# Pool's K and V loads as one transfer per kv-head, even heads first

## The chip, the cores and the metric

The kernel runs on one core of one Trainium2 chip. The metric is the device time of one execution in microseconds; the time before is the median of three runs. A profile of one execution, with its trace, stands beside the times.

## The reference

One decode step (one token, batch of 4) of an attention block and a GeGLU block that share a layer norm and are added to the input, together with the gradients of everything. With `D` = 512, 32 query heads, 8 kv-heads, `Dh` = 128, a cache of 4096 rows of which the last `W` = 1024 are attended, and an FFN width of 1792, cut to what matters:

```python
def _A_ref(x, k_cache, v_cache, wq, wo):
    W = min(4096, max(256, Sk // 4))
    q = (x @ wq).reshape(B, Sq, Hq, Dh).transpose(0, 2, 1, 3)
    k = jnp.repeat(k_cache[:, :, Sk - W:, :], rep, axis=1)
    v = jnp.repeat(v_cache[:, :, Sk - W:, :], rep, axis=1)
    p = softmax(einsum("bhqd,bhkd->bhqk", q, k) * Dh ** -0.5)
    return einsum("bhqk,bhkd->bhqd", p, v).transpose(0, 2, 1, 3).reshape(B, Sq, Hq * Dh) @ wo
def _B_ref(x, w_gate, w_up, w_down):
    return (gelu(x @ w_gate) * (x @ w_up)) @ w_down
xn = layernorm(x)
y = x + _A_ref(xn, k_cache, v_cache, wq, wo) + _B_ref(xn, w_gate, w_up, w_down)
# outputs: y, and the gradients for x, k_cache, v_cache, wq, wo, w_gate, w_up, w_down under grad_out
```

All tensors are bf16. The gradients of the caches have the caches' full shape, 32 MiB each. Outside of the window of 1024 rows they are zero, so 48 MiB of zeros are written; inside it stand dK and dV, 16 MiB in all. The kernel reads the windows of K and V, 8 MiB each.

## The kernel before, in words

The program works in three stages. First comes the FFN, forward and backward, with its weight gradients; in the meantime `wq`, `wo` and the first batch's K arrive on SP's queue. Then comes the attention, one batch after another. At the end are the projections' outputs and the gradients of `wo` and `wq`, in eight stores of 1 MiB.

K and V of a batch are tiles of 128 partitions by 8 kv-heads by 8 rows by 128 columns (2 MiB). A partition `m` holds the 8 consecutive cache rows `8m` to `8m+7` of each head, so one head is 2 KB on each partition, and one contiguous 256 KB in the cache. The pieces of a batch's work, in the names that the prediction uses:

- `load_kv` (L216) allocates the tile and issues its transfers (L222) at high priority. The first K load (`ka`) is issued by SP; the other seven by Pool (GpSimd): V of all four batches (`va`, one buffer), K of batches 1 to 3 (`kb`, `ka`, `kb`). The V load of the next batch waits until TensorE has finished its products with the old V (`odq`, tile `od_ps`), as it takes the same buffer; K loads wait likewise.
- `refill` (L462) copies the query rows, or the rows of the output's gradient, into the block-diagonal operands `bd` (tiles `D3q` and `D3d` are the sources) on Pool. The four `bd` tiles are cleared by memsets (L392) on Pool before their first use.
- `scores` (L471) makes the products with K (`S`) or V (`dP`). VectorE transposes 32x32 blocks of the tile into a scratch tile (`scr`, two buffers, L93), and TensorE multiplies it with `bd` into `sc_ps`. There are four transposes for a tile: two over the even heads, then two over the odd ones.
- `softmax`, `turned`, `odq` and `softmax_d` make the probabilities, the outputs and the gradient of the scores. `odq` reads the K or V tile head by head.
- `dvdk` (L550) makes dV or dK of a batch: products into `kv_ps`, copies by ScalarE and VectorE (`evac`, L88 and L89) into two of the four staging buffers `stg`, and two stores of 1 MiB each on Pool's queue (`result`, L106). A staging buffer can be written again when its store has landed.
- `zeros` (L236) issues the zero stores, 32 of 1.5 MiB, on SP's queue. Their order is written out by hand (SP is the only engine whose order is): a zero store waits for the landing of the second or third one before it, and in many places for the landing of the load that `load_kv` returned, which is the last transfer that it created:

```python
zeros(2, load_kv(0, 1, att, "va", nc.gpsimd, single_packet=True))
zeros(3, load_kv(1, 0, att, "kb", nc.gpsimd, single_packet=True))
```

The order on the other engines, Pool among them, is made by the Tile scheduler from priorities and a model of costs; each engine then runs its instructions in that order. Semaphores are assigned afterwards by Tile: landings of Pool's transfers are counted on eight semaphores taken in turn.

Of the kernel before, what the change touches and what calls it, by code (L numbers as in the profile page):

```python
# [18 lines left out]
def kernel(  # L19
# [24 lines left out]
    nc = tc.nc  # L44

    B, Sq, D = A_x.shape
    _, G, Sk, Dh = A_k_cache.shape
# [168 lines left out]
    def load_kv(b, k, pool, tag, eng, **kw):  # L216
        d_, src = ((k_t, A_k_cache), (v_t, A_v_cache))[k]
        tl = pool.tile([P, G, J, Dh], BF16, name=tag, tag=tag)
        for hf in range(2):
            hs = slice(hf * G // 2, (hf + 1) * G // 2)  # L220
            with tc.high_priority():
                d = eng.dma_start(out=tl[:, hs].rearrange("p g j d -> p g (j d)"),  # L222
                                  in_=src[b, hs, K0:Sk, :].rearrange("g (m j) d -> m g (j d)", j=J), **kw)
        d_[b] = tl
        return d
# [23 lines left out]
    with tc.tile_pool(name="ffn", bufs=1) as ffn:  # L249
# [17 lines left out]
        nc.sync.dma_start(out=wq_sb[:].rearrange("p c n -> p (c n)"), in_=A_wq.rearrange("(p c) n -> p (c n)", c=C))  # L267
        nc.sync.dma_start(out=wo_sb[:].rearrange("p k n -> p (k n)"), in_=A_wo.rearrange("(p k) n -> p (k n)", k=KH))
        load_kv(0, 0, kap, "ka", nc.sync)
        zeros(4)  # L270

# [103 lines left out]
    with tc.tile_pool(name="mid", bufs=1, reuse_waits="tile") as mid:  # L375
# [3 lines left out]
        selb = mid.tile([Q, 4, P], BF16, name="selb")  # L379
        with tc.tile_pool(name="att", bufs=1, reuse_waits="tile") as att:  # L380
            zeros(2, load_kv(0, 1, att, "va", nc.gpsimd, single_packet=True))
            zeros(3, load_kv(1, 0, att, "kb", nc.gpsimd, single_packet=True))


# [381 lines left out]
```

## Time and profile before

| What | Value |
|---|---|
| Median of 3 runs | 285.05 us (284.68 to 286.16) |
| The profiled execution | 284.82 us, span 283.0 us, 4400 instructions |
| Bytes moved | 112.21 MB, mean 396 GB/s over the span |
| Read and written in HBM | 30.93 MB and 81.01 MB |
| Pool's loads (`va`, `kb`, `ka`) | 8 + 4 + 2 transfers of 1024 KB, median 17.6, 19.4 and 13.0 us from issue to landing |
| Stores of dK, dV and the last two gradients | 24 of 1024 KB, median 13.7 us |
| Zero stores | 32 of 1536 KB, median 12.1 us |
| Granted TensorE clock, mean | 0.603 |

Rows of a timeline are: start in us, duration in us, engine, line, operation, output and input tiles, shape, number of instructions, and in brackets the idle time before it and what ended that. A "q" behind an engine's name is its sequencer. The queues' rows are packets, MB, and the time that the packets took as a share of sixteen DMA engines over the span (q1 is SP's, q0 Pool's). The slices divide the span into 40 equal parts, each digit a busy share in tenths.

### The profile page before, as it was taken

The page shows a single profiled execution, that of the slowest core. Times are in us where ns is not written, and L with a number is a line of the kernel's source. Part 1 is how long each engine was busy: PE and PEld are TensorE (multiplying, and loading weights), DVE is VectorE, ACT ScalarE, POOL GpSimd, SP SyncE. Part 2 cuts the span into 40 slices and gives each one's busy share as a digit, 9 for nine tenths or more (in the row PEclk, how much of TensorE's full clock was granted, in tenths as well). Part 3 has the DMA queues.
Part 4 walks back from the last instruction along what each step waited for, and adds up shares of the span by engine and source line. Part 5 has one row for each costly group of instructions (what it writes and reads, how often), then busy time and mean ns, then how long its engine had stood idle before and what let it go on. Part 6 is the DMA issues. An engine that isn't in the chain of part 4 may idle for free.

```text
span 283.0 us, 4400 instructions
## 1 busy us (share of the span) xinstructions
PE 187.6 (66%) x1731; PEld 76.8 (27%) x1733; DVE 165.0 (58%) x309; ACT 124.4 (44%) x245; POOL 60.3 (21%) x135
## 2 busy tenths in 40 slices
PE   0225989859544899759976663923357998944870
PEld 0102344233111543234331341311034232510210
DVE  4779674898798533635257254055496104396970
ACT  2032774740010469744725420802432767454870
POOL 8500000169075313120040060200020020201110
PEclk9999965556955555755555555555555555685555
DMA  6999989999999999999999999999999999999995
GB/s 217 430 446 435 432 317 420 424 430 396 392 428 406 383 357 425 328 365 411 421 419 414 408 427 405 396 422 421 429 382 423 413 410 403 399 415 396 391 397 223
DMA packets 16883, 112.21 MB, mean 396 GB/s; under 512 B 1368, under 2 KB 1632, under 8 KB 11104
## 3 DMA queue, kind: packets, MB, share of 16 engines
q1 hardware_dynamic: 6544, 66.46, 57.0%
q0 software_dynamic: 10176, 45.35, 40.8%
q8 instruction: 13, 0.21, 0.3%
q10 hardware_dynamic: 144, 0.13, 0.2%
q14 instruction: 6, 0.05, 0.0%
HBM read 30.93 MB, written 81.01 MB: 396 GB/s over the span
## 4 chain that ended last, share of the span: by engine, by line
DMA 30%; issue 14%; PE 13%; DVE 9%; ACT 3%; POOL 2%; POOLq 0%; ACTq 0%; DVEq 0%
DMA out_dram<-stg 30%; DVE scr L93 4%; PE kv_ps L117 4%; PE od_ps L117 3%; PE sc_ps L117 2%; PE dwq_ps L117 2%; ACT stg L88 2%; DVE stg L89 1%; POOL out_dram L106 1%; PE ok_ps L117 1%; PE es_ps L117 1%; DVE spr L492 1%; DVE dqs L593 1%; ACT E_f L524 1%; PE nm_ps L117 1%
## 5 line engine op out<-in xcount | busy, mean ns | idle before, releaser
L88 ACT CAST stg<-kv_ps 128x512 bf16<-128x512 f32 x118 | 63.6, 606 | 52.2 <-DMA out_dram<-stg 26.3
L106 POOL DMA_DIRECT2D out_dram<-stg x30 | 19.7, 659 | 150.0 <-ACT stg L88 94.7
L117 PE MATMUL sc_ps<-scr,bd 128*32 128x256 bf16 x256 | 24.2, 396 | 15.2 <-DVE scr L93 15.2
L117 PE MATMUL kv_ps<-qm,spr 32*128 32x256 bf16 x128 | 24.8, 385 | 13.0 <-ACT stg L88 12.5
L117 PE MATMUL kv_ps<-dm,spr 32*128 32x256 bf16 x128 | 28.9, 399 | 6.6 <-ACT stg L88 4.9
L93 DVE STREAM_TRANSPOSE scr<-va 128x1024 uint32<-128x1024 uint32 x16 | 18.9, 1219 | 12.9 <-DMA va<-in_A_v_cache_dram 12.8
L117 PEld LDWEIGHTS <-spr 32*128 32x128 bf16 x256 | 12.4, 102 | 46.4 <-issue 42.1
L89 DVE CAST stg<-kv_ps 128x512 bf16<-128x512 f32 x10 | 6.6, 683 | 17.0 <-PE kv_ps L117 11.0
L117 PEld LDWEIGHTS <-bd 128*32 128x32 bf16 x256 | 8.1, 107 | 29.1 <-issue 28.5
L88 ACT CAST stg<-dwg_ps 128x448 bf16<-128x448 f32 x26 | 12.7, 554 | 6.4 <-PE dwg_ps L117 5.5
L88 ACT CAST stg<-dwo_ps 128x512 bf16<-128x512 f32 x18 | 10.0, 588 | 11.4 <-PE dwo_ps L117 10.1
L117 PE MATMUL dwo_ps<-dy_b,oSP 32*128 32x512 bf16 x32 | 9.0, 508 | 7.5 <-ACT stg L88 6.2
L93 DVE STREAM_TRANSPOSE scr<-ka 128x1024 uint32<-128x1024 uint32 x8 | 9.6, 1228 | 5.2 <-DMA ka<-in_A_k_cache_dram 3.1
L222 POOL DMA_DIRECT2D va<-in_A_v_cache_dram x8 | 6.0, 757 | 27.3 <-PE od_ps L117 25.8
L93 DVE STREAM_TRANSPOSE scr<-kb 128x1024 uint32<-128x1024 uint32 x8 | 9.8, 1232 | 3.5 <-DMA kb<-in_A_k_cache_dram 2.9
L117 PE MATMUL do_ps<-scr,dyBD 128*128 128x512 bf16 x31 | 10.1, 459 | 2.4 <-DVE scr L93 2.1
L578 DVE SCALAR_TENSOR_TENSOR odt<-od_ps,oms,odt 128x128 f32<-128x128 f32 x4 | 1.4, 340 | 17.0 <-ACT odt L577 17.0
L117 PE MATMUL dwq_ps<-dqSP,xn_b 32*128 32x512 bf16 x32 | 10.7, 586 | 0.9 <-ACT stg L88 0.3
L89 DVE CAST stg<-dwq_ps 128x512 bf16<-128x512 f32 x15 | 9.9, 689 | 1.6 <-PE dwq_ps L117 1.4
L89 DVE CAST stg<-dwo_ps 128x512 bf16<-128x512 f32 x14 | 9.2, 680 | 2.7 <-PE dwo_ps L117 2.7
L117 PEld LDWEIGHTS <-pT 128*32 128x32 bf16 x256 | 9.2, 140 | 5.2 <-ACT pT L88 2.3
L88 ACT CAST stg<-dwq_ps 128x512 bf16<-128x512 f32 x17 | 9.7, 586 | 1.4 <-PE dwq_ps L117 0.7
(196 smaller groups left out, 321.3 us busy)
## 6 DMA issues: line engine op xcount, KB each, us to landing
out_dram<-ztile SPq DMA_DIRECT2D x32, 1536.0 KB, 12.1
out_dram<-stg POOLq DMA_DIRECT2D x24, 1024.0 KB, 13.7
va<-in_A_v_cache_dram POOLq DMA_DIRECT2D x8, 1024.0 KB, 17.6
out_dram<-stg POOLq DMA_DIRECT2D x6, 896.0 KB, 10.2
wq_sb<-in_A_wq_dram SPq DMA_DIRECT2D x1, 4096.0 KB, 25.6
wo_sb<-in_A_wo_dram SPq DMA_DIRECT2D x1, 4096.0 KB, 36.7
kb<-in_A_k_cache_dram POOLq DMA_DIRECT2D x4, 1024.0 KB, 19.4
ka<-in_A_k_cache_dram SPq DMA_DIRECT2D x2, 1024.0 KB, 44.3
```

The source lines that it names most:

```text
L88: return nc.scalar.copy(out=out, in_=in_)
L89: return nc.vector.tensor_copy(out=out, in_=in_)
L93: nc.vector.transpose(out=out, in_=in_)
L106: d = eng.dma_start(out=out, in_=in_, **kw)
L117: nc.tensor.matmul(out, lhsT=lhsT, rhs=rhs, start=first, stop=last, **kw)
L222: d = eng.dma_start(out=tl[:, hs].rearrange("p g j d -> p g (j d)"), in_=src[b, hs, K0:Sk, :].rearrange("g (m j) d -> m g (j d)", j=J), **kw)
L492: TS(out=sp[:, :, a, :], in0=src[:].rearrange("p (j m) -> p j m", j=J), scalar1=amask[:, a:a + 1], scalar2=None, op0=ALU.mult)
L524: nc.scalar.activation(out=E_f[:], in_=S, func=ACT.Exp, bias=negm[:, 0:1], scale=1.0, accum_out=es[:])
L578: done = STT(out=t_[:], in0=ps[:, 1, :], scalar=mk[:, 1:2], in1=t_[:], op0=ALU.mult, op1=ALU.add)
L593: nc.vector.tensor_copy(out=dqs[q, :, :, :, a * B + b], in_=d3v[q])
```

## The change

Where Pool issues the load, the tile is loaded by eight transfers, one for each kv-head (128 rows of 2 KB), heads 0, 2, 4, 6 and then 1, 3, 5, 7. SP's load stays as two transfers of four heads. `load_kv` returns the last one created, so what `zeros` waits for becomes the transfer of head 7.

```diff
         tl = pool.tile([P, G, J, Dh], BF16, name=tag, tag=tag)
-        for hf in range(2):
-            hs = slice(hf * G // 2, (hf + 1) * G // 2)
+        parts = [slice(hf * G // 2, (hf + 1) * G // 2) for hf in range(2)]
+        if eng is nc.gpsimd:
+            parts = [slice(g, g + 1) for g in (*range(0, G, 2), *range(1, G, 2))]
+        for hs in parts:
             with tc.high_priority():
                 d = eng.dma_start(out=tl[:, hs].rearrange("p g j d -> p g (j d)"),
                                   in_=src[b, hs, K0:Sk, :].rearrange("g (m j) d -> m g (j d)", j=J), **kw)
```

## The prediction

> **What bounds the kernel now.** I read the page first: engines, slices, queues. None of the compute engines is full, while the DMA row is at 9 in every slice but the first and last, and the two data queues add up to 57.0 + 40.8 = 97.8% of the sixteen engines' time.
>
> ```profile
> PE 187.6 (66%) x1731; PEld 76.8 (27%) x1733; DVE 165.0 (58%) x309; ACT 124.4 (44%) x245; POOL 60.3 (21%) x135
> DMA  6999989999999999999999999999999999999995
> q1 hardware_dynamic: 6544, 66.46, 57.0%
> q0 software_dynamic: 10176, 45.35, 40.8%
> ```
>
> So time is lost where the DMA engines run dry, or move the same bytes less well; a wait of a compute engine counts only if it leads there. The zero stores on SP (q1) are the filler, and they are let go by landings of Pool's loads.
>
> Next, Pool's timeline. Its instructions run strictly in this order; the rows are start, duration, what, and the idle time before.
>
> ```profile
> 55.95 0.53 POOL L106 DMA_DIRECT2D out_dram<-stg  x1 [3.68 <-ACT stg L88]
> 58.06 1.52 POOL L222 DMA_DIRECT2D va<-in_A_v_cache_dram  x2 [1.57 <-PE dwg_ps L117]
> 60.33 1.49 POOL L222 DMA_DIRECT2D kb<-in_A_k_cache_dram  x2 [0.74 <-DVE scr L93]
> 61.81 0.56 POOL L106 DMA_DIRECT2D out_dram<-stg  x1
> 62.35 3.65 POOL L392 MEMSET bd<- 128x1024 bf16 x4
> ...
> 69.50 1.31 POOL L469 COPY bd<-D3q 32x64 bf16<-32x64 bf16 x6
> 79.33 1.75 POOL L469 COPY bd<-D3d 32x64 bf16<-32x64 bf16 x8 [8.52 <-DVE D3d L93]
> ...
> 97.38 1.50 POOL L222 DMA_DIRECT2D va<-in_A_v_cache_dram  x2 [2.21 <-PE od_ps L117]
> ```
>
> The block-diagonal operand `bd`, without which no score product can start, is cleared and filled from 62.35 to 70.81, right behind two loads and a store. Its first reader follows on TensorE's and VectorE's timelines:
>
> ```profile
> 77.69 1.25 DVE L93 STREAM_TRANSPOSE scr<-ka 128x1024 uint32<-128x1024 uint32 x1 [0.70 <-PE r_ps L117]
> 78.99 0.62 PE L117 MATMUL sc_ps<-scr,bd 128*32 128x256 bf16 x8 [1.34 <-DVE scr L93]
> 83.22 4.59 DVE L93 STREAM_TRANSPOSE scr<-va 128x1024 uint32<-128x1024 uint32 x4
> ```
>
> Pool has 78.99 - 70.81 = 8.2 us to spare there, no more. Last, the DMA view of the stretch 97.4 to 101.8, right after the second V load is issued:
>
> ```profile
> q1 hardware_dynamic: 130, 1.52, 99.9%
> ```
>
> All that moves are zeros already in flight; V's first bytes come at 101.8, as the zeros run out. The page's slices show no hole, but there is also no stock left.
>
> **What the change removes and adds.** Seven loads are Pool's (V of four batches, K of three), so 14 transfers become 56. Bytes and destinations stay.
>
> Issue time. A transfer of 512 rows holds Pool for 0.75 us, one of 128 rows (the store at 55.95) for 0.53. A load takes 8 x 0.53 = 4.24 instead of 1.50, 2.7 more. The first head goes out earlier than the first half did, and a store behind a load is served after it in the queue anyway. I take 0; without that cover 2.7 for each load on the path.
>
> Waits. Landings are counted on eight semaphores in turn: in the compiled program of before, each Pool transfer from the ninth on is preceded by a wait for the landing of the Pool transfer eight places earlier. With 44 transfers that one had always long landed, so the profile shows no Pool wait on a DMA. With eight transfers a load it binds. Count the stores at 32.56 to 55.95 as 1 to 5. V's heads are 6 to 13, K's 14 to 21, the store of 61.81 is 22. Transfer 13 waits for 5, the store of 55.95, which lands 12.9 us after its start, at 68.9. Transfer 14 waits for V's first head, 21 for its eighth, and 22 for the first K head. V's two halves land 16.6 and 18.6 us after 58.06 and 58.82, at 74.7 and 77.4; the queue is first in, first out and never empty, so V is still complete at 77.4. K's first half lands 19.7 after 60.33, at 80.0; a quarter of these 2.6 us gives its first head at 78.1. The store is out at 78.7 in place of 62.35, and queued behind it on Pool are the memsets and fills, 8.46 us long: done at 87.2, with the fill that the first product needs 0.2 sooner.
>
> Who waits: TensorE, from 78.99 to 87.0. VectorE has two scratch buffers, so it stops after two K transposes, resumes at 87.6, needs 2 x 1.2 for the others and starts V's at 90.0 in place of 83.22: the whole chain (softmax, products, the second V load) is 6.8 late, and that load goes out at 104.2. Zeros ran out at 101.8 as V's bytes arrived, so a lag of 6.8 is up to 6.8 of dry DMA. From below: with nothing else moving, a Pool transfer may start sooner than 4.4 us after its issue; the last store of the kernel lands 5.5 us after its start, 2.6 of them its 1 MiB at 397 GB/s, so start and end take 2.9 together, and V begins by 107.1, 5.3 dry. I take 6.0. DMA is full from there on, so nothing gives this back. No stall shorter than it can hide: stores and loads up to 187 us hang on this chain, and ACT's waits for store landings (28.2 us in all) move with the DMA.
>
> The other waits of this kind (a K or V head behind a store of the batch before, from 111 us on) fall on heads that stand behind that store in the same queue, with seven transfers in it: 0. One fill (165.67) slips behind them to about 182; its reader is the V transpose at 187 or later, still covered.
>
> Zeros. They wait for the load's last created transfer. At 97.38 this was the half that was issued first, and two zeros went at 105.76; after, it may be the last head. That is 0 to 2.8 us without zeros, mostly filled by a store: I take 0.5.
>
> Packets. Of q0's 10176 records, 44 x 16 are completions, 768 and 1024 belong to stores of 7 and 8 KB rows; the remaining 7680 carry thirty transfers of 1 MiB, so 4096 B each: two rows of 2 KB. Whether rows of two partitions are still joined, nothing shows. If not, the records say 84 ns for 2048 B (SP's own K load) against 160 for 4096: 64 x 84 - 32 x 160 = 0.26 us for each load, 1.8 for seven. Queues also take turns packet by packet (from 188 to 196 us, 224 packets of q0 and 225 of q1), so a load beside 12 KB zeros would get 2/14 of the engines in place of 4/16, and the stores behind it land later, worth 0 to 3. From the other side, loads run slower than stores (395 GB/s from 72 to 80, 429 from 188 to 196), and a head is one contiguous 256 KB where a half took strides: 14.7 MB at 429 in place of 395 would save 2.9. I take 0, nearest to the same records.
>
> The Trainium skill's page "DMA: Bandwidth & Descriptors" (Anatomy of one DMA — SWDGE (gpsimd) path) speaks against small transfers: about 2.0 us fixed beside bytes at 436 GB/s, estimated 2.6 us for a head and 4.4 for a half. Paid one after the other that would be 20.8 against 8.8, or 84 us over seven loads, 369 us in all. The trace disagrees for queued transfers: V's halves land 2.7 us apart, less than one 4.4, so the fixed part overlaps.
>
> What the change gives: products on even heads may start before the odd heads land. VectorE waits for loads 12.8 + 3.1 + 2.9 = 18.8 us, five times; at most 2 x 1.2 each, 12 in all, could go. With DMA full it only waits elsewhere: 0.
>
> Sum: 6.0 + 0.5 = 6.5 on the profiled execution's 284.8 (span 283.0 and 1.8 around it) gives 291.3; the median of the runs is 0.2 above that execution, hence 291.5.
>
> **Rivals.** (B) The same lag and 2 KB packets: 1.8 + 0 to 3 more, 293 to 297. For it: SP's K load moves 2 KB records; against: Pool's joins two. (C) Pool's order changes with the number of transfers, memsets and fills ahead of the heads; no lag remains, 285 to 286. Against: in the profile Pool held the fills back even for the 0.74 us that K's load waited. (D) Faster, by one mechanism: one-head reads are served at the stores' rate, in the seven loads. 2.9 us, 282; it decides only if the lag at 79 us stays under about 1.5, which needs C's order too.
>
> **How the numbers follow.** A 0.48, B 0.30, C 0.13 (0.11 of it no change), D 0.09. A measurement here tells about 0.5%, 1.4 us, from none. Slower 0.48 + 0.30 + 0.02 = 0.80, same 0.11, faster 0.09. Likeliest case alone: 289.5 to 294.5. The range drops D, C's lower half and B's far end: 285 to 298.
>
> **What would show it.** Pool's timeline: K's heads strung out to about 77 us, the `bd` memsets after 78, the first score product near 87; the second V load near 104 and a DMA hole of 5 to 7 us before its bytes. q0's packets: 10176 + 42 x 16 = 10848 with 4 KB, 14432 with 2 KB. If the memsets stay near 62 and the time still rises, the reason is wrong; if the hole is there and the time is not, DMA had slack that I did not see.

## The result and the profile after

The changed kernel takes 292.33 us (median of 6 runs, 291.53 to 294.12) against 284.90 us for the kernel before on the same chip (6 runs, 284.55 to 286.66). The ratio is 1.0267, 95% interval 1.0231 to 1.0303. The profiled execution took 292.20 us, its span is 290.4 us, 7.4 more than before. Its whole timeline starts some 1.2 us earlier than before's (the store ahead of V's first load starts at 54.71, before at 55.95), which has to be kept in mind where start times are compared. Some kernels below had an execution in a slower state of the chip; their medians include it, the ratios leave it out.

The page of after: slices and the two data queues.

```profile
DMA  6999989999999859999999999999979999999996
q1 hardware_dynamic: 6544, 66.46, 55.8%
q0 software_dynamic: 10848, 45.36, 40.4%
```

The sixteen engines are less full: 96.2% in place of 97.8%. Two slices stand out, the fifteenth (5) and the thirtieth (7). q0 has 10848 packets, exactly the 672 more that 42 further transfers bring as completions; the rows of 2 KB are still joined to 4096 B.

Pool's timeline from the first V load to the second (start, duration, what, and in brackets the idle time before):

```profile
56.81 1.62 POOL L224 DMA_DIRECT2D va<-in_A_v_cache_dram  x3 [1.58 <-PE dwg_ps L117]
59.08 1.07 POOL L224 DMA_DIRECT2D kb<-in_A_k_cache_dram  x2 [0.65 <-DVE scr L93]
...
66.38 0.54 POOL L224 DMA_DIRECT2D kb<-in_A_k_cache_dram  x1 [5.18 <-DMA out_dram<-stg]
68.86 0.54 POOL L224 DMA_DIRECT2D kb<-in_A_k_cache_dram  x1 [1.94 <-DMA va<-in_A_v_cache_dram]
71.77 0.54 POOL L224 DMA_DIRECT2D va<-in_A_v_cache_dram  x1 [2.37 <-DMA va<-in_A_v_cache_dram]
...
76.24 0.54 POOL L224 DMA_DIRECT2D kb<-in_A_k_cache_dram  x1
77.23 0.54 POOL L106 DMA_DIRECT2D out_dram<-stg  x1 [0.45 <-ACT scr L420]
77.76 3.65 POOL L394 MEMSET bd<- 128x1024 bf16 x4
84.91 1.31 POOL L471 COPY bd<-D3q 32x64 bf16<-32x64 bf16 x6
103.22 4.24 POOL L224 DMA_DIRECT2D va<-in_A_v_cache_dram  x8 [2.21 <-PE od_ps L117]
```

The transfers wait for landings of a store and of V's heads ("<-DMA" in the brackets), and the memsets of `bd` stand behind them, at 77.76 in place of 62.35. TensorE and VectorE pay for it:

```profile
86.09 1.05 PE L117 MATMUL sc_ps<-scr,bd 128*32 128x256 bf16 x16 [9.67 <-POOL bd L471]
89.05 4.58 DVE L93 STREAM_TRANSPOSE scr<-va 128x1024 uint32<-128x1024 uint32 x4
```

Around the second V load the DMA engines stand still. The columns of this view are the window, its length, busy time (and instructions) of PE, PEld, DVE, ACT and POOL, the granted clock, the busy share of the DMA engines, and GB/s:

```profile
100.00:101.00 1.00, 0.40 (x9) 0.35 (x12) 1.00 (x4) 0.37 (x1) 0.82 (x4) 0.50 0.57 234
101.00:102.00 1.00, 1.00 (x27) 0.88 (x20) 1.00 (x5) 0.00 (x0) 0.01 (x1) 0.50 0.06 16
102.00:103.00 1.00, 1.00 (x21) 0.49 (x16) 0.80 (x1) 0.04 (x1) 0.00 (x0) 0.50 0.00 0
103.00:104.00 1.00, 0.68 (x10) 0.24 (x2) 0.35 (x1) 0.86 (x3) 0.78 (x2) 0.50 0.00 0
104.00:105.00 1.00, 1.00 (x6) 1.00 (x7) 0.00 (x0) 1.00 (x4) 1.00 (x3) 0.50 0.17 61
105.00:106.00 1.00, 1.00 (x9) 0.98 (x8) 0.23 (x1) 0.52 (x2) 1.00 (x3) 0.50 1.01 401
```

How much of the 7.4 us is that hole? The same view by stretches, of the kernel before:

```profile
95.00:110.00 15.00, 14.55 (x146) 6.62 (x142) 5.16 (x16) 10.10 (x21) 3.34 (x8) 0.50 1.01 391
110.00:205.00 95.00, 61.08 (x605) 26.69 (x597) 44.89 (x89) 42.11 (x89) 14.34 (x25) 0.52 1.01 405
205.00:225.00 20.00, 15.27 (x177) 7.18 (x173) 12.89 (x27) 8.55 (x19) 1.50 (x2) 0.50 0.99 405
```

and of after:

```profile
95.00:110.00 15.00, 11.48 (x153) 7.01 (x153) 7.85 (x23) 6.37 (x14) 7.20 (x21) 0.50 0.72 257
110.00:205.00 95.00, 58.92 (x612) 24.82 (x611) 40.37 (x80) 43.23 (x90) 26.26 (x50) 0.52 1.01 397
205.00:225.00 20.00, 11.96 (x131) 6.23 (x131) 15.12 (x22) 7.56 (x16) 1.50 (x2) 0.50 0.92 370
```

At some 400 GB/s the bytes not moved are worth 15 x (391 - 257) / 400 = 5.0 us in the first stretch, 95 x 8 / 400 = 1.9 in the second, and 20 x 35 / 400 = 1.8 in the third. Together 8.7; the rest of the span gives back 1.3. (This is a rough account: the same window holds somewhat different work in the two kernels.) So there are three losses: the hole that was forecast, a second, small hole near 215 us, and a long stretch in which the engines are always busy and still move 2% less. The second hole, in after:

```profile
214.00:215.00 1.00, 0.88 (x6) 0.70 (x4) 1.00 (x4) 0.58 (x1) 0.02 (x1) 0.50 0.51 209
215.00:216.00 1.00, 0.32 (x2) 0.00 (x0) 1.00 (x2) 0.65 (x2) 0.73 (x1) 0.50 0.01 4
```

### The profile page after: what moved, and what is told of

The parts are those of the page before. It is cut to its first block, busy times and chain, and to the rows that moved or that the text cites. A ratio compares the mean times of both kernels' runs of the same rounds, so it can differ in the third digit from the quotient of the medians.

```text
span 290.4 us, 4460 instructions
## 1 busy us (share of the span) xinstructions
PE 186.2 (64%) x1733; PEld 75.1 (26%) x1733; DVE 165.1 (57%) x309; ACT 124.6 (43%) x245; POOL 79.8 (27%) x177
## 3 DMA queue, kind: packets, MB, share of 16 engines
q0 software_dynamic: 10848, 45.36, 40.4%
## 4 chain that ended last, share of the span: by engine, by line
DMA 23%; PE 16%; issue 14%; DVE 9%; POOL 5%; ACT 5%; POOLq 0%; DVEq 0%; ACTq 0%
DMA out_dram<-stg 19%; DVE scr L93 5%; PE kv_ps L117 5%; DMA va<-in_A_v_cache_dram 4%; PE sc_ps L117 4%; ACT stg L88 3%; PE dwq_ps L117 2%; PE od_ps L117 2%; DVE stg L89 1%; POOL va L224 1%; POOL bd L394 1%; POOL out_dram L106 1%; PE ok_ps L117 1%; PE dwo_ps L117 1%; PE es_ps L117 1%
## 5 line engine op out<-in xcount | busy, mean ns | idle before, releaser
L93 DVE STREAM_TRANSPOSE scr<-va 128x1024 uint32<-128x1024 uint32 x16 | 18.8, 1215 | 26.3 <-DMA va<-in_A_v_cache_dram 26.2
L117 PE MATMUL kv_ps<-dm,spr 32*128 32x256 bf16 x128 | 27.2, 392 | 1.7 <-DVE spr L494 1.5
L224 POOL DMA_DIRECT2D va<-in_A_v_cache_dram x32 | 17.1, 541 | 25.9 <-PE od_ps L117 16.4
L117 PEld LDWEIGHTS <-spr 32*128 32x128 bf16 x256 | 11.7, 102 | 42.7 <-issue 38.3
L117 PE MATMUL dwo_ps<-dy_b,oSP 32*128 32x512 bf16 x32 | 10.0, 546 | 6.1 <-ACT stg L88 5.2
L224 POOL DMA_DIRECT2D kb<-in_A_k_cache_dram x16 | 8.6, 538 | 19.2 <-DMA out_dram<-stg 13.5
L117 PE MATMUL dqr_ps<-odt,rsum 128*128 128x128 f32 x8 | 3.2, 501 | 14.0 <-DVE odt L580 13.8
L526 ACT ACTIVATE E_f<-sc_ps,negm 128x256 f32<-128x256 f32 x4 | 1.9, 474 | 21.3 <-DVE negm L523 21.3
```

Of the source, the lines that this page charges most:

```text
L93: nc.vector.transpose(out=out, in_=in_)
L117: nc.tensor.matmul(out, lhsT=lhsT, rhs=rhs, start=first, stop=last, **kw)
L526: nc.scalar.activation(out=E_f[:], in_=S, func=ACT.Exp, bias=negm[:, 0:1], scale=1.0, accum_out=es[:])
```

## The experiments

Every kernel ran with the kernel before on the same chip; ratios are to that.

### Heads for the later five loads alone

```diff
-        if eng is nc.gpsimd:
+        if eng is nc.gpsimd and (k, b) not in ((1, 0), (0, 1)):
```

> The first two Pool loads (V of batch 0, K of batch 1) go as two halves again, the later five stay at eight heads. Theory (the 16 heads of the first two loads hold back the clearing and filling of the score operand by some 15 us, and the lag lets the DMA run dry once): the fills end near 71 us, the second V load goes out near 97, no dry stretch before it, time 284.5 to 287. Rival (small transfers and the eight-back waits cost wherever they stand): five of seven loads still pay, so about five sevenths of the 7.4 us stay, 289 to 291.

285.40 us (10 runs), ratio 0.9988 (0.9948 to 1.0028). By themselves, thirty of the 42 added transfers cost nothing that can be told. With the first two loads as halves the memsets start at 61.34, the second V load goes out at 96.21, and 95 to 110 us moves 372 GB/s. The waits on landings are there all the same, in its table of waits (total, times, longest):

```profile
POOL va L224 <- DMA out_dram<-stg: 13.3, 2, 8.6
```

As long as nothing else is late, they are hidden.

### Heads for the first two loads alone

```diff
-        if eng is nc.gpsimd:
+        if eng is nc.gpsimd and (k, b) in ((1, 0), (0, 1)):
```

> The complement: only the first two Pool loads go as eight heads, the later five as two halves. Theory: the whole lag of about 6 us stays, 290 to 292. Rival: two sevenths of 7.4, 286.5 to 287.5. If this run and the one with the later five add up to the 7.4 us of the full change, the two parts are independent.

289.01 us (4 runs), ratio 1.0120 (1.0059 to 1.0181): between the two ranges, below the theory's 290 to 292. Memsets at 77.50, second V load at 102.97, and the same hole: 281 GB/s from 95 to 110 us. Sixteen transfers are enough for it. But the two parts don't add up: 1.2% and nothing, together 2.67%. The 1.6 percentage points between (0.8 to 2.4 with the three intervals) appear only when late fills and the later heads meet.

### The kernel before, with the memsets held back

```diff
-                    nc.gpsimd.memset(t_[:], 0.0)
+                    behind(nc.gpsimd.memset(t_[:], 0.0).ins, v_0.ins)
```

(the same on the memsets of `selh` and `dqs`; `v_0` is what the first V load returns)

> The kernel before, with its 14 Pool transfers, but the memsets of the score operand on Pool wait for the landing of the first V load's second half (near 77 us), as they come to stand in the changed kernel. Theory: the wait alone makes the loss: first score product near 86 to 87, second V load near 103, DMA dry for 4 to 6 us, 290 to 292. Rival (the number and size of the transfers make the loss): 284.5 to 286.

296.19 us (4 runs), ratio 1.0386 (1.0322 to 1.0451), with the 14 transfers and 10176 packets of before.

```profile
80.83 3.62 POOL L393 MEMSET bd<- 128x1024 bf16 x4 [20.09 <-DMA va<-in_A_v_cache_dram]
106.28 1.50 POOL L222 DMA_DIRECT2D va<-in_A_v_cache_dram  x2 [2.21 <-PE od_ps L117]
```

The lag alone, without one more transfer, costs time: 209 GB/s from 95 to 110. It is more than was expected and more than the change itself cost. In part that is a longer lag: V's second half was put behind K's halves, so the memsets came 3.1 us later than in after, and the second V load too. In part the engines stood still again, at 114 to 116 us (8 GB/s), and from 110 to 205 us they moved 380 GB/s, before 405.

### Even and odd heads as two transfers

```diff
-            parts = [slice(g, g + 1) for g in (*range(0, G, 2), *range(1, G, 2))]
+            parts = [slice(0, G, 2), slice(1, G, 2)]
```

> Even heads first without more transfers: each Pool load is one transfer of the four even heads and one of the four odd ones. Theory: nothing is held back on Pool, and as the compiled program lets the first transpose of a tile wait for both transfers (a range from head 0 to head 6 is taken to touch heads 1, 3 and 5 too), VectorE gains nothing: 284 to 286. Rival (even heads first is worth something when it costs Pool nothing): VectorE's waits for loads shrink by up to 2.4 us each, 280 to 284.

284.56 us (10 runs), ratio 0.9975 (0.9942 to 1.0008): no difference that can be told. VectorE waited 12.2 + 6.7 + 3.3 = 22.2 us for loads, before 18.8. The compiled program says why it can't be less: the even heads of a tile are read with a stride, the dependence is taken over the whole range from head 0 to head 6, and the first transpose waits for both transfers (in the changed kernel for seven of the eight).

### Even and odd heads as two blocks of the tile

So the layout was changed too: even heads in the tile's first half, odd ones in its second, the even transfer always issued first.

```diff
+            hs, ds = slice(hf, G, 2), slice(hf * G // 2, (hf + 1) * G // 2)
...
-                        ... src[:, g2:G:2, :, e * Q:(e + 1) * Q], 1024)
+                        ... src[:, g2 * NQ:(g2 + 1) * NQ, :, e * Q:(e + 1) * Q], 1024)
...
-                        mm(..., src[:, 2 * c:2 * c + 2, j, :], ...)
+                        mm(..., src[:, c:c + 5:4, j, :], ...)
```

> The purpose of the change, carried out: two transfers a load, even heads and odd heads, laid out in the tile as a block of four even heads and a block of four odd ones, and the even one issued first, so that the first two transposes wait for the even transfer alone. 14 transfers, no lag. Theory (VectorE's waits for loads lie beside a full DMA): these waits fall from 18.8 us by 4 to 12, and the time stays, 283.6 to 285.8, ratio 0.995 to 1.003. Rival (products that start sooner bring the next loads sooner and are worth time): 281 to 283, ratio under 0.993.

288.61 us (8 runs), ratio 1.0083 (1.0045 to 1.0120), slower than either theory had it, and VectorE waited 24.0 + 6.9 + 6.1 = 37.0 us for loads, not less. The zeros were now behind the odd transfer, the last one out, and DMA ran dry when it had landed:

```profile
106.00:107.00 1.00, 1.00 (x12) 0.34 (x10) 0.72 (x1) 1.00 (x3) 0.33 (x1) 0.50 0.16 61
107.00:108.00 1.00, 1.00 (x10) 0.21 (x7) 0.41 (x1) 1.00 (x4) 0.43 (x1) 0.50 0.00 0
```

### The same, with the zeros behind the even transfer

```diff
-        return d
+        return ds_[0]
```

(`ds_` holds the two transfers)

> Even and odd heads as two blocks and two transfers, the even one first, as in the run before, but the zeros behind a load wait for the even transfer, the first one out, not for the odd one. There DMA stood nearly still from 105.8 to 108, since all heads had landed before the zeros were let go. Theory (the late gate made that kernel 0.8% slower): the hole is gone, 284 to 286, ratio 0.996 to 1.003. Rival (the interleaving of the first V and K transfers or the earlier products cost it): still 287.5 to 289, ratio above 1.006.

286.22 us (12 runs), ratio 1.0037 (1.0000 to 1.0073), at the upper end of the theory's range, just above it. The hole is gone:

```profile
106.00:107.00 1.00, 1.00 (x10) 0.34 (x9) 1.00 (x1) 0.03 (x1) 0.15 (x1) 0.50 1.16 467
107.00:108.00 1.00, 1.00 (x13) 0.26 (x9) 0.07 (x1) 0.99 (x3) 0.00 (x0) 0.50 1.01 406
```

The hole came from the late gate, that is, from zeros that wait for the load's last landing. What it cost is less sure: the two ratios, from different chips, are 0.46 points apart, with both intervals -0.06 to 0.98. And the purpose of the change, carried out in this way, gains nothing: products may start on half a tile, VectorE gets there sooner, and waits 32.9 us for loads where it had waited 18.8.

### All 56 transfers, the second K load behind the first fills

```diff
-            zeros(3, load_kv(1, 0, att, "kb", nc.gpsimd, single_packet=True))
...
+            filled = refill(0, 0)
+            with tc.issue_after(filled.ins):
+                k_1 = load_kv(1, 0, att, "kb", nc.gpsimd, single_packet=True)
+            zeros(3, k_1)
```

(`refill` returns its last copy)

> All 56 transfers, but the eight of the second K load are put behind the first eight fills of the block-diagonal operand on Pool, so that the memsets and these fills do not stand behind them. Theory (the lag of the fills makes the whole loss): memsets begin by 68, the fills end by 76, first score product near 79, 285 to 287, ratio 1.000 to 1.008. Rival (the smaller transfers cost by themselves, wherever they stand): 289 to 292, ratio above 1.012.

289.99 us (4 runs), ratio 1.0161 (1.0116 to 1.0206): in the rival's range. Still it doesn't decide, as the lag was not taken away whole. V's seventh and eighth heads themselves wait on Pool, 0.76 and 5.24 us, for stores to land, so the memsets start at 70.78 and not by 68; and K's load, at 79.47 in place of 60.33, leaves the engines dry around 91 (33 and 0 GB/s from 90 to 92). A loss was exchanged for another one.

### Four transfers of two heads

```diff
+            parts = [slice(g, g + 3, 2) for g in (0, 4, 1, 5)]
```

> A half dose: each of Pool's loads as four transfers of two heads, heads 0 and 2, 4 and 6, 1 and 3, 5 and 7; 28 transfers in place of 56. The store ahead of the memsets now waits for the landing of V's first pair, not of a K head. Theory (the lag decides): V's first pair lands near 70, the memsets begin at 69 to 73, the fills end at 78 to 82 and the first score product starts 0 to 3 us later than before, 285 to 287.5, ratio 1.000 to 1.010. Rival (each transfer costs by itself): half of the change's loss, 288 to 289.5, ratio 1.011 to 1.016.

289.53 us (4 runs), ratio 1.0124 (1.0064 to 1.0185): the value in the rival's range, the interval reaching into both. The memsets start at 73.71, the last of the first eight fills ends at 82.40, 11.6 later than before where 8.2 were to spare, and the second V load is out at 101.24, 3.9 later. The lag was larger than expected, so the run doesn't separate the two. The profiled execution was itself 293.06 us, above the other three (288.09 to 289.93), so these start times are rough.

### Where do the late fills and the later heads meet? The second V load

The first idea was this load's zeros. The scheduler had put head 7, on which they wait, first of its eight: zeros were let go at 106.20, after an eighth of the load, and the other heads shared the engines with them and were whole only at 118.1 (before: 109.2). Two kernels tested it. One lets these zeros wait for heads 4 and 7 (`ds` collects the eight transfers, and `zeros` takes a list):

```diff
-        return d
+        return [ds[2], ds[-1]] if eng is nc.gpsimd and k == 1 and b > 0 else d
```

> The changed kernel, with one edit: the zeros behind the V loads of batches 1 to 3 wait for the transfers of heads 4 and 7, not of head 7 alone. In the changed kernel head 7 of the second V load was issued first, so zeros were let go at 106.2 after an eighth of the load and the other heads shared the engines with them until 118.1. Theory (the late load and the early zeros work together): zeros go after the fourth head, V is whole by 113 to 115, and the time falls from 292.3 to 289 to 291, a ratio of 1.012 to 1.020 to the kernel before. Rival (what came on top of the 3.4 us of the first two loads is something else): V whole at 118 as before or earlier without gain, 291.5 to 293, ratio 1.023 to 1.031.

294.20 us (4 runs), ratio 1.0301 (1.0242 to 1.0359). V was whole at 114.0, 4.1 us earlier, and the time did not fall. The other one uses heads for the first three loads only:

```diff
+        if eng is nc.gpsimd and (k, b) in ((1, 0), (0, 1), (1, 1)):
```

> Heads for the first V and K load and the second V load alone, halves for the other four. Theory (the rest of the loss is made at the second V load, which comes late and shares with zeros): V whole near 118, 291 to 292.5, ratio 1.021 to 1.028. Rival (each of the later loads adds a little): near the kernel with heads for the first two loads, 289 to 290, ratio 1.012 to 1.017.

289.90 us (4 runs), ratio 1.0148 (1.0102 to 1.0195): V whole at 119.3, and the loss is hardly more than with two loads. Both missed the idea's range; that idea fell. The second run is the cleaner of the two, as in the first one a later stretch was slower too (340 GB/s from 205 to 225 us, in after 370).

### Where do they meet? The third V load

In after's trace ScalarE's longest wait on a DMA is for a staging buffer, in front of the softmax of batch 2. Pool's timeline shows the store of that buffer behind the third V load:

```profile
134.48 3.75 POOL L224 DMA_DIRECT2D va<-in_A_v_cache_dram  x7 [7.01 <-PE od_ps L117]
142.41 0.54 POOL L224 DMA_DIRECT2D va<-in_A_v_cache_dram  x1 [4.18 <-DMA out_dram<-stg]
145.66 0.76 POOL L106 DMA_DIRECT2D out_dram<-stg  x1 [2.71 <-ACT pT L88]
```

and ScalarE's:

```profile
160.89 2.54 ACT L88 CAST stg<-kv_ps 128x512 bf16<-128x512 f32 x5 [11.19 <-DMA out_dram<-stg]
```

The eighth head waits for the landing of the store eight places before it (142.12 in the trace). The next store's data were ready by 128.2, when the last copy for it ended; in the compiled program it is preceded by a wait for the landing of the load's first head, which came at 145.08. (The row names ScalarE's `pT` as the releaser. That is only the event nearest in time; the program waits for no such thing.) The store lands at 160.86, and ScalarE, which executes in order, holds all behind it for 11.19 us; the fourth V load goes out at 172.77 in place of 162.63. Again two kernels, opposite ways. The change without heads for this one load:

```diff
+        if eng is nc.gpsimd and (k, b) != (1, 2):
```

> The changed kernel with one load, the third V load, as two halves again; the other six stay eight heads. In the changed kernel this load's eighth head waited on Pool from 138.2 to 142.4 for the landing of the store of 126.7, a dK store stood behind it until 145.7 and landed at 160.9, and ScalarE waited 11.2 us for that buffer. Theory (these later waits on landings make the second part of the loss, because the chain is late already): that store goes out near 137, ScalarE's wait is under 5 us, the fourth V load goes out by 169 in place of 172.8, the time falls to 288.5 to 290.5, ratio 1.010 to 1.018. Rival (the second part is made elsewhere): 291.5 to 293, ratio 1.022 to 1.030.

290.36 us (4 runs), ratio 1.0169 (1.0119 to 1.0220). Its rows, of Pool, of ScalarE and of the third stretch:

```profile
136.29 0.76 POOL L106 DMA_DIRECT2D out_dram<-stg  x1
156.29 2.54 ACT L88 CAST stg<-kv_ps 128x512 bf16<-128x512 f32 x5 [3.90 <-DMA out_dram<-stg]
205.00:225.00 20.00, 15.39 (x178) 6.78 (x177) 11.54 (x23) 8.70 (x17) 1.38 (x2) 0.50 1.01 416
```

The store goes out 9.4 us sooner, the wait shrinks to 3.90, the fourth V load goes out at 170.12 (a little later than expected), and the second hole is gone. The ratio falls by 0.98 points; with both intervals taken together that is 0.4 to 1.6. The counterpart adds heads for this load to those of the first two:

```diff
+        if eng is nc.gpsimd and (k, b) in ((1, 0), (0, 1), (1, 2)):
```

> Heads for the first V and K load and for the third V load, halves for the other four: the counterpart. The eighth head of the third V load waits on Pool for the landing of the dK store before it, and the next dK store stands behind it. Theory (as above): 290 to 292, ratio 1.016 to 1.026, ScalarE's wait for the staging buffer near 10 us. Rival (that wait is hidden): as with heads for the first two loads alone, 288.5 to 289.5, ratio 1.010 to 1.014.

290.74 us (4 runs), ratio 1.0184 (1.0125 to 1.0244), in the theory's range, but its interval touches the rival's, and it is not told apart from heads for the first two loads alone (0.6 points more, -0.2 to 1.5). The wait is 7.84 us, not 10. A second dry stretch is there and comes sooner than in after: 262, 172 and 90 GB/s in the three us from 190 to 193. But heads for the first two loads alone have a smaller one too (317 and 283 GB/s in the two stretches from 209 to 213), so these heads can make a late chain worse, and are not needed for it to run dry again.

The table shows GB/s by stretch, from the profiles, beside the ratios.

| Heads for | Ratio | Second V load out | 95 to 110 | 110 to 205 | 205 to 225 |
|---|---|---|---|---|---|
| none (before) | 1 | 97.38 | 391 | 405 | 405 |
| later five | 0.9988 | 96.21 | 372 | 400 | 413 |
| first two | 1.0120 | 102.97 | 281 | 404 | 393 |
| first three | 1.0148 | 103.29 | 248 | 400 | 422 |
| first two and third V | 1.0184 | 103.27 | 286 | 395 | 411 |
| all but third V | 1.0169 | 103.29 | 256 | 401 | 416 |
| all (after) | 1.0267 | 103.22 | 257 | 397 | 370 |

No version tried is faster than the kernel before by more than a measurement can tell.

## Why the prediction held, step by step

**The outcome.** 292.33 against 291.5 predicted, within 285 to 298 and within the likeliest case's own 289.5 to 294.5. The lag, which carries the forecast, was right. But its price was taken too large, and losses that were put at 0 made up for it, so that the number came out within 0.8 us is partly luck.

**The waits and the lag: right.** Fills end at 86.22 (87.2 predicted), the first product starts at 86.09 (87.0), V's transposes at 89.05 (90.0), the second V load at 103.22 (104.2). All are 1.0 early, on a timeline that is itself 1.2 early; against before it is a lag of 103.22 - 97.38 + 1.24 = 7.1 us, 6.8 predicted. The order was foreseen less well: V's and K's heads go out interleaved, and not even heads first. The kernel held back with 14 transfers has the hole, the one with heads for the later five loads, 44 transfers in all, has not: the lag is the cause, not the number of transfers.

**The dry stretch: right in place, too large.** 6.0 was taken, between 5.3 and 6.8. The rows of 100 to 106 us give some 4.2 without bytes, from about 100.6 to 104.85. The step that was mis-sized is the start of a Pool transfer into an idle queue: 2.9 us was the least allowed, from issue at 103.22 it took 1.6.

**The other waits of this kind, 0: wrong in the changed kernel.** Alone they cost nothing, as the run with the later five loads shows. On top of a late chain they do: the wait at the third V load holds a store and with it ScalarE for 11.19 us, and the chain is so late by 214 us that DMA runs dry a second time. Without heads for that load this hole is gone, and 0.98 points of the 2.67 with it. That this wait alone makes the second hole is not shown, as heads for the first two loads alone have a small one. The step's reason, that the waits fall on "heads that stand behind that store in the same queue", looked at the head that waits, and not at the next store behind it and the engine that needs that store's buffer. "DMA is full from there on, so nothing gives this back" was nearly right in that little was given back, and wrong in that it could get worse.

**Zeros, 0.5: not seen in after.** At the second V load the zeros waited for the head that was issued first, so they came early. What a late gate does is shown by the two block kernels: a hole of some 2 us with it and none without, at 1.0083 and 1.0037.

**Packets: 0 for the number, open for the rate.** 10848 packets, so rival B's 2 KB packets did not happen. Yet from 110 to 205 us after moves 397 GB/s and before 405, at a full share in both: 1.9 us. The table has 395 to 401 wherever three loads or more came as heads and 404 to 405 in the two others, but this is one profile each, and with heads for the first three loads most of the stretch runs on halves and still has 400. Nor does a low rate need small transfers: with 14 transfers the first block kernel has 389 GB/s there, at a share of 1.00. It was not isolated, and it stays open.

**Issue time, 0: right.** Eight issues take 4.24 us (row at 103.22), and the kernel with heads for the later five loads lost nothing. The Trainium skill's page "DMA: Bandwidth & Descriptors" (Anatomy of one DMA — SWDGE (gpsimd) path), from whose fit the prediction worked out an estimate of 369 us if fixed costs were paid one after another, is answered by the heads of batch 3's K load: in after's trace the eight land 0.66 to 0.68 us apart, 256 KB each, about 390 GB/s, so queued transfers don't pay the fixed part one after another.

**The even heads first, 0: right, but the step's premise was not.** Products on even heads could not start before the odd heads landed: the scheduler permutes the heads, and the first transposes wait for seven of the eight. Where neither holds (the block kernels) the gain is still none, as the step's reason, a full DMA, has it.

**The rivals.** C (another order on Pool) and D (faster reads) did not happen; the order did change, but not to the memsets' favour.

## What to carry to other kernels

Splitting a transfer multiplies what is queued behind its completion count: with eight landing semaphores in turn, eight pieces make the next transfer on that engine wait for the one eight places back, and with it all that stands behind on the engine, so look first at what stands behind the load on the issuing engine (here the memsets, and later a store whose buffer ScalarE needed). A wait that costs nothing while the chain is on time can cost once something else is late, so such costs are to be tried together and not summed. And a filler that was released by the last landing of a load left a hole behind it here; an early part of the load was the better release.

## What the runs showed of the hardware and the compiled program, unexpected

- A Pool transfer into an idle queue moved its first bytes about 1.6 us after its issue began (103.22 to some 104.85). The Trainium skill's page "DMA: Bandwidth & Descriptors" (Latency and other measured facts) gives about 1 us to the first byte on this path, which is what is left here when it is counted from the end of the 0.53 us that the issue takes.
- With the zeros released by the last landing of a load, the engines stood still for some 1.8 us (106 to 108 us in the first block kernel: 61 and 0 GB/s) until the released transfers' bytes came.
- A strided read of a tile counted as a read of all between its first and last element: the first transposes waited for odd heads that they don't read.
- Transfers of equal priority were issued in an order unlike the program's: the heads of the second V load as 7, 3, 2, 4, 0, 5, 6, 1.
